# A Fourier-filter-and-snake-MLP kernel: forward transform with both sample parities in one 512-column matmul, and the filter's product in 512-wide pairs

## The chip, the cores and the metric

The kernel runs on one core of a Trainium2 chip. The metric is the device time of one execution in microseconds (us). TensorE (PE in the profile, PEld for its weight loads) multiplies, VectorE (DVE) and ScalarE (ACT) work elementwise, GpSimd (POOL) here issues the DMAs that change type, and SyncE (SP) issues the other DMAs.

## The reference, cut to what matters

The input has 8 batches of 3008 positions and 256 channels. Each batch is filtered along its positions by a real Fourier transform, and the result goes through a two-layer network with a snake activation:

```
X = np.fft.rfft(x, axis=1)
Y = X * (filt_r + 1j * filt_i)[None, :, :]
y = np.fft.irfft(Y, n=x.shape[1], axis=1)
h = y.reshape(B * S, D) @ w_in                 # 256 -> 2048
s = np.sin(alpha * h)
g = h + s * s / (alpha + 1e-09)
out = g @ w_out                                # 2048 -> 256
```

## The kernel before

The transform of length 3008 is split by parity. The even positions (r = 0) and the odd ones (r = 1) each have a transform of length 1504, done as matmuls with a table of cosines and sines, `dt_t`, that stays on the chip. 753 frequencies are kept, as 6 blocks of 128 (index i). Real and imaginary parts are p = 0 and p = 1. The odd half's twiddle factor and the filter are folded into coefficient tables once, at the start: P0 is the filter's even part, Q0 and P1 its odd part times the twiddle, each with a real and an imaginary table.

For each batch b:

- **x** is loaded (L205, L210) by GpSimd's queue, f32 to f16, into one tile for each parity, positions on the partitions in 12 chunks k (the last has 96 rows). The tile pool has two buffers of each.
- **Forward** (L226, L229): for each block i, part p and chunk k, one matmul 128x256 for the even samples into `psA` and one for the odd samples into `psB`, with the same weights `dt_t` loaded twice. 48 matmuls for one i, 288 for a batch. A PSUM tile of 512 columns holds both parts of one parity.
- **Copies** (L234, L235): ScalarE turns `psA` and `psB` into f16 tiles `asb` and `bsb` (two buffers each).
- **Product** (L247 to L253): VectorE forms four results z for each i, one for each output parity r and part p. Each takes four multiplications and three additions or subtractions of 128x256, 28 instructions for one i, 168 for a batch. The z tiles have one buffer.
- **Inverse** (L261): for each output parity r, 72 matmuls of 512 or 480 columns from z and the table `e_t` into `psy`, summed over all i and p; ScalarE copies them to `y` (L267).
- **Network** (L273 to L306): `psh` is y times w_in, ScalarE takes the sine, VectorE squares it in place (`v`, L283), and `pso` sums v times w_out (L292) and y times w_in·w_out (L299). VectorE copies `pso` to `o` and SyncE stores it.

At the start, VectorE makes the coefficient tables, for each i after a reversal of the filter on TensorE (`psrev`, L155) that VectorE copies out (L156, L157). The tiles of this part give their memory to those of the main loop, so the first load of x waits for all of it.

A scheduler sets the order on each engine from its own estimates, and each engine then keeps to that order. Between the last blocks of `pso` of one batch it places single forward matmuls of the next batch. Semaphores make an instruction wait for its operands.

Of the kernel before, what the change touches and what calls it, by code (L numbers as in the profile page):

```python
# [17 lines left out]
def kernel(  # L18
# [61 lines left out]
    P0re = cpool.tile([128, 6, C], FP16)  # L80
    P0im = cpool.tile([128, 6, C], FP16)
    Q0re = cpool.tile([128, 6, C], FP16)
    Q0im = cpool.tile([128, 6, C], FP16)
    P1re = cpool.tile([128, 6, C], FP16)
    P1im = cpool.tile([128, 6, C], FP16)
# [11 lines left out]
    with tc.tile_pool(name="init", bufs=1) as ipool:  # L97
# [68 lines left out]
        for i in range(6):  # L166
            wv = w3_t[:, 0, i:i + 1]
            wcv = w3_t[:, 1, i:i + 1]
            wsv = w3_t[:, 2, i:i + 1]
            nc.vector.tensor_tensor(out=gre, in0=fr_f[:, i, :], in1=fr_b[:, i, :], op=ALU.add)  # L170
            nc.vector.tensor_tensor(out=hre, in0=fr_f[:, i, :], in1=fr_b[:, i, :], op=ALU.subtract)
            nc.vector.tensor_tensor(out=gim, in0=fi_f[:, i, :], in1=fi_b[:, i, :], op=ALU.subtract)
            nc.vector.tensor_tensor(out=him, in0=fi_f[:, i, :], in1=fi_b[:, i, :], op=ALU.add)
            if i == 0:
                nc.vector.memset(gim[0:1, :], 0.0)
                nc.vector.memset(him[0:1, :], 0.0)
            nc.vector.tensor_scalar(out=P0re[:, i, :], in0=gre, scalar1=wv, scalar2=None, op0=ALU.mult)
# [5 lines left out]
            nc.vector.tensor_tensor(out=Q0re[:, i, :], in0=ta, in1=tb, op=ALU.add)
            nc.vector.tensor_tensor(out=Q0im[:, i, :], in0=tc_, in1=td, op=ALU.subtract)
            nc.vector.tensor_tensor(out=P1re[:, i, :], in0=ta, in1=tb, op=ALU.subtract)
            nc.vector.tensor_tensor(out=P1im[:, i, :], in0=tc_, in1=td, op=ALU.add)
# [10 lines left out]

    tok_chunks = [(0, 512), (512, 512), (1024, 480)]

    for b in range(B):  # L200
        xr_tiles = []
        for r in range(2):
            xt = xpool.tile([128, 12, C], FP16, name=f"x_{b}_{r}", tag=f"x{r}")
            base = x.offset + b * S * C + r * C
            nc.gpsimd.dma_start(  # L205
                out=xt[:, 0:11, :],
                in_=bass.AP(tensor=x.tensor, offset=base,
                            ap=[[2 * C, 128], [256 * C, 11], [1, C]]),
            )
            nc.gpsimd.dma_start(  # L210
                out=xt[0:96, 11, :],
                in_=bass.AP(tensor=x.tensor, offset=base + 1408 * 2 * C,
                            ap=[[2 * C, 96], [1, C]]),
            )
            xr_tiles.append(xt)
        Z = [[zpool.tile([128, 6, C], FP16, name=f"z_{b}_{r}_{p}", tag=f"z{r}{p}") for p in range(2)]
             for r in range(2)]
        for i in range(6):
            psA = fwdps.tile([128, 2, C], FP32, name=f"psA_{b}_{i}", tag="psA")
            psB = fwdps.tile([128, 2, C], FP32, name=f"psB_{b}_{i}", tag="psB")  # L220
            for p in range(2):
                col0 = p * NQP + 128 * i
                for k in range(12):
                    nrow = 128 if k < 11 else 96
                    lhs = dt_t[0:nrow, k, col0:col0 + 128]
                    nc.tensor.matmul(out=psA[:, p, :], lhsT=lhs,  # L226
                                     rhs=xr_tiles[0][0:nrow, k, :],
                                     start=(k == 0), stop=(k == 11))
# [7 lines left out]
            are, aim = asb[:, 0, :], asb[:, 1, :]
            bre, bim = bsb[:, 0, :], bsb[:, 1, :]
            t0 = abpool.tile([128, C], FP16, name=f"t0_{b}_{i}", tag="t0")
            t1 = abpool.tile([128, C], FP16, name=f"t1_{b}_{i}", tag="t1")
            for (zout, ops, c0, x0, c1, x1, c2, x2, c3, x3) in (  # L240
                (Z[0][0][:, i, :], 0, P0re, are, P0im, aim, Q0re, bre, Q0im, bim),
                (Z[0][1][:, i, :], 1, P0re, aim, P0im, are, Q0re, bim, Q0im, bre),
                (Z[1][0][:, i, :], 0, P1re, are, P1im, aim, P0re, bre, P0im, bim),
                (Z[1][1][:, i, :], 1, P1re, aim, P1im, are, P0re, bim, P0im, bre),
            ):
                sub = ALU.add if ops else ALU.subtract
# [96 lines left out]
```

## Time and profile before

| | |
|---|---|
| median of 5 runs | 1392.18 us (1391.09 to 1395.18) |
| profiled execution | 1390.42 us, of which the span from first to last instruction is 1388.6 us |
| PE busy | 1277.8 us (92%), 8524 matmuls |
| DVE busy | 752.8 us (54%), 2453 instructions |
| ACT busy | 562.8 us (41%), 962 instructions |
| DMA | mean 40 GB/s, q0 (GpSimd's) 24848 packets, 13.37 MB |
| mean granted clock of TensorE | 0.977 |

The busy times are sums over the whole span. The ends of matmuls are modelled and matmuls overlap, so a stretch of PE is read by the starts of its instructions. An idle time in the trace is the gap in front of an instruction, and the name behind it is what ended it.

### The profile page before, as it was taken

What the parts mean: (1) busy time and instruction counts of PE and PEld (TensorE: products, weight loads), DVE (VectorE), ACT (ScalarE), POOL (GpSimd) and SP (SyncE); (2) the same over time, 40 slices, a digit from 0 to 9 for tenths busy, and PEclk for the clock granted to TensorE, in tenths of its full rate; (3) what the DMA queues carried; (4) which work ended last, traced back from release to release, by engine and by line L of the source; (5) the groups of instructions that cost most, each with busy time, mean ns of one, the idle gap of its engine ahead of it and who ended that gap; (6) DMA issues with size and microseconds to landing.
All of it is one profiled execution on the core that took longest, in us unless ns stands there. A gap on an engine that the chain in (4) does not pass through costs nothing.

```text
span 1388.6 us, 21372 instructions
## 1 busy us (share of the span) xinstructions
PE 1277.8 (92%) x8524; PEld 819.1 (59%) x8524; DVE 752.8 (54%) x2453; ACT 562.8 (41%) x962; POOL 33.2 (2%) x53
## 2 busy tenths in 40 slices
PE   0629899989999999999999899998999999999998
PEld 0208465765568465775658565684657655684655
DVE  0757644495256753495355753486444952566534
ACT  0002546316361454416362264514463164613544
POOL 0110000000000000000000000000000000000000
PEclk9859999999999999999999999999999999999999
DMA  9542310030000310121000300103100000000101
GB/s 335 165 67 39 52 38 16 31 45 24 23 31 16 45 35 21 35 34 27 30 24 23 46 31 15 39 10 50 38 16 30 2 23 23 31 15 1 35 19 38
DMA packets 60501, 56.21 MB, mean 40 GB/s; under 512 B 6129, under 2 KB 59633, under 8 KB 59889
## 3 DMA queue, kind: packets, MB, share of 16 engines
q1 hardware_dynamic: 35552, 41.48, 8.6%
q0 software_dynamic: 24848, 13.37, 7.1%
q8 instruction: 66, 1.08, 0.4%
q14 instruction: 35, 0.28, 0.1%
HBM read 43.57 MB, written 24.64 MB: 49 GB/s over the span
## 4 chain that ended last, share of the span: by engine, by line
PE 72%; DVE 21%; SPq 2%; DMA 2%; issue 1%; ACT 1%; POOL 0%; ACTq 0%; DVEq 0%; POOLq 0%
PE pso L292 26%; PE psh L273 24%; PE psy L261 15%; PE pso L299 3%; DVE t L250 3%; DVE t L252 3%; DVE t L247 3%; DVE z L253 3%; DVE t L249 3%; DVE t L248 3%; DVE t L251 3%; SPq L99 2%; PE psB L229 2%; PE psA L226 1%; DMA tfwd<-in_filt_i_dram 1%
## 5 line engine op out<-in xcount | busy, mean ns | idle before, releaser
L279 ACT ACTIVATE v<-psh,alpha_t 128x512 f16<-128x512 f32 (+1 forms) x768 | 453.2, 718 | 174.5 <-PE psh L273 172.4
L283 DVE TENSOR_TENSOR v<-v 128x512 f16<-128x512 f16 (+1 forms) x768 | 321.4, 419 | 311.4 <-ACT v L279 285.5
L292 PE MATMUL pso<-w_out,v 128*128 128x256 f16 (+1 forms) x3072 | 443.6, 273 | 2.1 <-DVE o L306 1.5
L273 PE MATMUL psh<-y,w_in 128*128 128x512 f16 (+1 forms) x1536 | 418.2, 374 | 1.4 <-ACT v L279 1.4
L292 PEld LDWEIGHTS <-v 128*128 128x128 f16 (+1 forms) x3072 | 301.8, 99 | 180.9 <-DVE v L283 81.0
L261 PE MATMUL psy<-e_t,z 128*128 128x512 f16 (+1 forms) x1152 | 264.8, 382 | 29.2 <-DVE z L253 28.5
L226 PE MATMUL psA<-x,dt_t 128*128 128x256 f16 (+1 forms) x1152 | 255.4, 275 | 20.0 <-DMA x<-in_x_dram 20.0
L229 PE MATMUL psB<-x,dt_t 128*128 128x256 f16 (+1 forms) x1152 | 255.3, 274 | 1.1 <-DMA x<-in_x_dram 1.1
L273 PEld LDWEIGHTS <-w_in 128*128 128x128 f16 x1536 | 149.3, 97 | 101.2 <-issue 20.0
L261 PEld LDWEIGHTS <-z 128*128 128x128 f16 x1152 | 112.2, 99 | 161.8 <-DVE z L253 44.0
L306 DVE COPY o<-pso 128x256 f32<-128x256 f32 x192 | 81.5, 425 | 217.6 <-PE pso L299 217.3
L267 ACT CAST y<-psy 128x512 f16<-128x512 f32 (+1 forms) x96 | 54.6, 578 | 259.3 <-PE psy L261 259.3
L226 PEld LDWEIGHTS <-dt_t 128*128 128x128 f16 (+1 forms) x1152 | 112.9, 98 | 35.8 <-issue 21.6
L234 ACT CAST asb<-psA 128x512 f16<-128x512 f32 x48 | 28.1, 586 | 248.6 <-PE psA L226 136.5
L229 PEld LDWEIGHTS <-dt_t 128*128 128x128 f16 (+1 forms) x1152 | 113.5, 99 | 15.7 <-issue 1.4
L299 PE MATMUL pso<-m_t,y 128*128 128x256 f16 (+1 forms) x384 | 73.3, 273 | 0.0
L253 DVE TENSOR_TENSOR z<-t,t 128x256 f16<-128x256 f16 x192 | 54.6, 288 | 2.7
L249 DVE TENSOR_TENSOR t<-t,t 128x256 f16<-128x256 f16 x192 | 54.4, 286 | 1.8
L251 DVE TENSOR_TENSOR t<-t,t 128x256 f16<-128x256 f16 x192 | 54.4, 286 | 1.8
L247 DVE TENSOR_TENSOR t<-P0re,asb 128x256 f16<-128x256 f16 x96 | 27.5, 286 | 43.2 <-ACT asb L234 42.7
L119 PE MATMUL pst<-ident_t,w_in 128*128 128x128 f32 x32 | 10.6, 404 | 39.5 <-DMA w_in<-in_moe_w_in_dram 37.8
L234 ACT ACT_TABLE_LOAD x1 | 1.3, 1283 | 110.1 <-PE psA L226 110.1
(45 smaller groups left out, 378.2 us busy)
## 6 DMA issues: line engine op xcount, KB each, us to landing
out_dram<-o SPq DMA_DIRECT2D x176, 128.0 KB, 1.7
x<-in_x_dram POOLq DMA_DIRECT2D x16, 704.0 KB, 9.5
dt_t<-dt_tbl SPq DMA_DIRECT2D x1, 4608.0 KB, 15.6
e_t<-e_tbl SPq DMA_DIRECT2D x1, 4512.0 KB, 28.7
w_in<-in_moe_w_in_dram SPq DMA_DIRECT2D x1, 2048.0 KB, 7.5
w_out<-in_moe_w_out_dram SPq DMA_DIRECT2D x1, 2048.0 KB, 13.1
out_dram<-o SPq DMA_DIRECT2D x16, 96.0 KB, 1.7
w_in<-in_moe_w_in_dram POOLq DMA_DIRECT2D x1, 1024.0 KB, 28.9
```

The source lines that it names most:

```text
L226: nc.tensor.matmul(out=psA[:, p, :], lhsT=lhs, rhs=xr_tiles[0][0:nrow, k, :], start=(k == 0), stop=(k == 11))
L229: nc.tensor.matmul(out=psB[:, p, :], lhsT=lhs, rhs=xr_tiles[1][0:nrow, k, :], start=(k == 0), stop=(k == 11))
L249: nc.vector.tensor_tensor(out=t0, in0=t0, in1=t1, op=sub)
L251: nc.vector.tensor_tensor(out=t0, in0=t0, in1=t1, op=ALU.add)
L253: nc.vector.tensor_tensor(out=zout, in0=t0, in1=t1, op=sub)
L261: nc.tensor.matmul(out=psy[:, 0:n], lhsT=Z[r][p][:, i, cb * 128:cb * 128 + 128], rhs=e_t[:, p, i, m0:m0 + n], start=(i == 0 and p == 0), s ...
L273: nc.tensor.matmul(out=psh[:, 0:n], lhsT=w_in16[:, cb, jb * 128:jb * 128 + 128], rhs=ysb[:, cb, m0:m0 + n], start=(cb == 0), stop=(cb == 1),)
L279: nc.scalar.activation(out=vt[:, jb, 0:n], in_=psh[:, 0:n], func=AFT.Sin, scale=alpha_t[:, jb:jb + 1],)
L283: nc.vector.tensor_tensor(out=vt[:, jb, 0:n], in0=vt[:, jb, 0:n], in1=vt[:, jb, 0:n], op=ALU.mult,)
L292: nc.tensor.matmul(out=pso[0:tn, 0:C], lhsT=vt[:, jb, 128 * t:128 * t + tn], rhs=w_out2[:, jb, :], start=(jb == 0), stop=False,)
L299: nc.tensor.matmul(out=pso[0:tn, 0:C], lhsT=ysb[:, cb, m0 + 128 * t:m0 + 128 * t + tn], rhs=m_t[:, cb, :], start=False, stop=(cb == 1),)
L306: nc.vector.tensor_copy(out=osb[0:tn, :], in_=pso[0:tn, 0:C])
```

## The change

The two parity tiles of x become one tile of 12 chunks with 2 x 256 columns, loaded in rows twice as long. A forward matmul now has 512 columns, both parities at once, and the two PSUM tiles hold the real part and the imaginary part (`psRE`, `psIM`) instead of the even and the odd samples. There are 24 forward matmuls for one i instead of 48. The coefficient tables are stored side by side (`CR`, `CI`: for r = 0 [P0 | Q0], for r = 1 [P1 | P0]), which takes 12 more VectorE instructions at the start. A result z is now made by two multiplications and one addition or subtraction of 128x512 and one addition of 128x256: 16 instructions for one i instead of 28. The load of x for the next batch is written one batch ahead.

```
-            nc.vector.tensor_scalar(out=P0re[:, i, :], in0=gre, scalar1=wv, scalar2=None, op0=ALU.mult)
-            nc.vector.tensor_scalar(out=P0im[:, i, :], in0=gim, scalar1=wv, scalar2=None, op0=ALU.mult)
+            nc.vector.tensor_scalar(out=CR[0][:, i, 0, :], in0=gre, scalar1=wv, scalar2=None, op0=ALU.mult)
+            nc.vector.tensor_scalar(out=CR[1][:, i, 1, :], in0=gre, scalar1=wv, scalar2=None, op0=ALU.mult)
+            nc.vector.tensor_scalar(out=CI[0][:, i, 0, :], in0=gim, scalar1=wv, scalar2=None, op0=ALU.mult)
+            nc.vector.tensor_scalar(out=CI[1][:, i, 1, :], in0=gim, scalar1=wv, scalar2=None, op0=ALU.mult)
...
+    def load_x(b):
+        xt = xpool.tile([128, 12, 2, C], FP16, name=f"x_{b}", tag="x")
+        base = x.offset + b * S * C
+        nc.gpsimd.dma_start(
+            out=xt[:, 0:11, :, :],
+            in_=bass.AP(tensor=x.tensor, offset=base,
+                        ap=[[2 * C, 128], [256 * C, 11], [1, 2 * C]]),
+        )
...
+    x_pref = load_x(0)
     for b in range(B):
...
+        xr = x_pref
+        if b + 1 < B:
+            x_pref = load_x(b + 1)
...
-                    nc.tensor.matmul(out=psA[:, p, :], lhsT=lhs,
-                                     rhs=xr_tiles[0][0:nrow, k, :],
+                    nc.tensor.matmul(out=pst, lhsT=dt_t[0:nrow, k, col0:col0 + 128],
+                                     rhs=xr[0:nrow, k, :, :],
                                      start=(k == 0), stop=(k == 11))
-                    nc.tensor.matmul(out=psB[:, p, :], lhsT=lhs,
-                                     rhs=xr_tiles[1][0:nrow, k, :],
-                                     start=(k == 0), stop=(k == 11))
...
-            nc.scalar.copy(out=asb, in_=psA)
-            nc.scalar.copy(out=bsb, in_=psB)
+            nc.scalar.copy(out=resb, in_=psRE)
+            nc.scalar.copy(out=imsb, in_=psIM)
...
-                nc.vector.tensor_tensor(out=t0, in0=c0[:, i, :], in1=x0, op=ALU.mult)
-                nc.vector.tensor_tensor(out=t1, in0=c1[:, i, :], in1=x1, op=ALU.mult)
-                nc.vector.tensor_tensor(out=t0, in0=t0, in1=t1, op=sub)
-                nc.vector.tensor_tensor(out=t1, in0=c2[:, i, :], in1=x2, op=ALU.mult)
-                nc.vector.tensor_tensor(out=t0, in0=t0, in1=t1, op=ALU.add)
-                nc.vector.tensor_tensor(out=t1, in0=c3[:, i, :], in1=x3, op=ALU.mult)
-                nc.vector.tensor_tensor(out=zout, in0=t0, in1=t1, op=sub)
+            for r in range(2):
+                for p in range(2):
+                    x0, x1 = (resb, imsb) if p == 0 else (imsb, resb)
+                    sub = ALU.add if p else ALU.subtract
+                    w0 = abpool.tile([128, 2, C], FP16, name=f"w0_{b}_{i}_{r}_{p}", tag="w0")
+                    w1 = abpool.tile([128, 2, C], FP16, name=f"w1_{b}_{i}_{r}_{p}", tag="w1")
+                    nc.vector.tensor_tensor(out=w0, in0=CR[r][:, i, :, :], in1=x0, op=ALU.mult)
+                    nc.vector.tensor_tensor(out=w1, in0=CI[r][:, i, :, :], in1=x1, op=ALU.mult)
+                    nc.vector.tensor_tensor(out=w0, in0=w0, in1=w1, op=sub)
+                    nc.vector.tensor_tensor(out=Z[r][p][:, i, :], in0=w0[:, 0, :], in1=w0[:, 1, :], op=ALU.add)
```

VectorE, product of batch 0, before. A name such as t0_0_1_576 is tile t0 of batch 0 and block 1; t0_0_0_492 belongs to block 0.

```order
L248 TENSOR_TENSOR t1_0_0_493<-P1im_69,asb_0_0_488 128x256
L247 TENSOR_TENSOR t0_0_1_576<-P0re_64,asb_0_1_572 128x256 [waits Activation_49]
L249 TENSOR_TENSOR t0_0_0_492<-t0_0_0_492,t1_0_0_493 128x256 [waits DVE_49]
L248 TENSOR_TENSOR t1_0_1_577<-P0im_65,asb_0_1_572 128x256
L250 TENSOR_TENSOR t1_0_0_493<-P0re_64,bsb_0_0_489 128x256 [waits DVE_49]
L249 TENSOR_TENSOR t0_0_1_576<-t0_0_1_576,t1_0_1_577 128x256 [waits DVE_49]
L251 TENSOR_TENSOR t0_0_0_492<-t0_0_0_492,t1_0_0_493 128x256 [waits DVE_49]
L250 TENSOR_TENSOR t1_0_1_577<-Q0re_66,bsb_0_1_573 128x256 [waits DVE_49,Activation_49]
```

The same place with the change: from the first product of block 1 that needs the imaginary part to the end of its first two results, and on to the third.

```order
L242 TENSOR_TENSOR w1_0_1_0_0_533<-CI0_66,imsb_0_1_529 128x512 [waits Activation_49]
L241 TENSOR_TENSOR w0_0_1_0_1_538<-CR0_64,imsb_0_1_529 128x512 [waits DVE_49]
L243 TENSOR_TENSOR w0_0_1_0_0_532<-w0_0_1_0_0_532,w1_0_1_0_0_533 128x512 [waits DVE_49]
L242 TENSOR_TENSOR w1_0_1_0_1_539<-CI0_66,resb_0_1_528 128x512
L244 TENSOR_TENSOR z_0_0_0_444<-w0_0_1_0_0_532 128x256 [waits DVE_49]
L243 TENSOR_TENSOR w0_0_1_0_1_538<-w0_0_1_0_1_538,w1_0_1_0_1_539 128x512 [waits DVE_49]
L241 TENSOR_TENSOR w0_0_1_1_0_544<-CR1_65,resb_0_1_528 128x512 [waits DVE_49]
L244 TENSOR_TENSOR z_0_0_1_445<-w0_0_1_0_1_538 128x256 [waits DVE_49]
L242 TENSOR_TENSOR w1_0_1_1_0_545<-CI1_67,imsb_0_1_529 128x512
```

Before, two blocks stood interleaved, so that an instruction's operand came from the second instruction ahead of it. With the change two results of one block stand interleaved, again at a distance of two.

TensorE, first inverse matmuls of batch 0, before, from the tenth on (psy_0_0_0_0 and psy_0_0_0_512 are the first two of the three column chunks of y).

```order
L261 LDWEIGHTS z_0_0_1_435 [waits DVE_49]
L261 MATMUL psy_0_0_0_512_957<-e_t_59,z_0_0_1_435 128x512
L261 LDWEIGHTS z_0_0_0_434 [waits DVE_49]
L261 MATMUL psy_0_0_0_0_943<-e_t_59,z_0_0_0_434 128x512
L261 LDWEIGHTS z_0_0_0_434
L261 MATMUL psy_0_0_0_512_957<-e_t_59,z_0_0_0_434 128x512
```

With the change, from the eleventh on:

```order
L252 LDWEIGHTS z_0_0_0_444
L252 MATMUL psy_0_0_0_512_787<-e_t_59,z_0_0_0_444 128x512
L252 LDWEIGHTS z_0_0_0_444 [waits DVE_49]
L252 MATMUL psy_0_0_0_0_773<-e_t_59,z_0_0_0_444 128x512
L252 LDWEIGHTS z_0_0_1_445
L252 MATMUL psy_0_0_0_512_787<-e_t_59,z_0_0_1_445 128x512
L252 LDWEIGHTS z_0_0_0_444
L252 MATMUL psy_0_0_0_512_787<-e_t_59,z_0_0_0_444 128x512
L252 LDWEIGHTS z_0_0_1_445 [waits DVE_49]
L252 MATMUL psy_0_0_0_0_773<-e_t_59,z_0_0_1_445 128x512
```

Before, 16 matmuls of other blocks stood ahead of the one that waits for the real z of block 5, and 10 more ahead of the one that waits for the imaginary z. Now 11 stand ahead of the first and 2 between the two.

GpSimd's queue, loads of x for batches 0 and 1, before:

```order
L210 DMA x_0_0_428<-in_x_dram 96x256
L205 DMA x_0_1_431<-in_x_dram 128x11x256
L210 DMA x_0_1_431<-in_x_dram 96x256
L205 DMA x_1_0_2126<-in_x_dram 128x11x256
L210 DMA x_1_0_2126<-in_x_dram 96x256
```

And with the change:

```order
L207 DMA x_0_438<-in_x_dram 96x512
L202 DMA x_1_441<-in_x_dram 128x11x512
L207 DMA x_1_441<-in_x_dram 96x512
L202 DMA x_2_1956<-in_x_dram 128x11x512 [waits DMASW2_49,DMASW1_49,PE_49]
L207 DMA x_2_1956<-in_x_dram 96x512
```

In both, two batches are asked for at once at the start, and the third waits for TensorE to be done with the first.

## Rows read from the trace of the kernel before

**Rows 1.** The page, part 4: shares of the chain that ended last

```profile
PE 72%; DVE 21%; SPq 2%; DMA 2%; issue 1%; ACT 1%; POOL 0%; ACTq 0%; DVEq 0%; POOLq 0%
```

**Rows 2.** Groups by line: busy us, mean ns of one, idle before and its releaser

```profile
L283 DVE TENSOR_TENSOR v<-v 128x512 f16<-128x512 f16 (+1 forms) x768 | 321.4, 419 | 311.4 <-ACT v L279 285.5
...
L261 PE MATMUL psy<-e_t,z 128*128 128x512 f16 (+1 forms) x1152 | 264.8, 382 | 29.2 <-DVE z L253 28.5
...
L235 ACT CAST bsb<-psB 128x512 f16<-128x512 f32 x48 | 28.2, 589 | 21.1 <-DVE t L252 21.1
```

**Rows 3.** Timeline, PE, batch 1: start us, us, line, count, idle before

```profile
267.38 0.27 PE L226 MATMUL psA<-x,dt_t 128*128 128x256 f16 x1
...
296.68 2.39 PE L261 MATMUL psy<-e_t,z 128*128 128x512 f16 x9
301.36 1.69 PE L261 MATMUL psy<-e_t,z 128*128 128x512 f16 x7 [2.28 <-DVE z L253]
...
307.38 9.63 PE L261 MATMUL psy<-e_t,z 128*128 128x512 f16 x45 [0.19 <-DVE z L253]
```

**Rows 4.** Timeline, VectorE, batch 1: interleaved, then dependent, then the last imaginary part

```profile
284.01 0.28 DVE L251 TENSOR_TENSOR t<-t,t 128x256 f16<-128x256 f16 x1
284.22 0.28 DVE L248 TENSOR_TENSOR t<-P0im,asb 128x256 f16<-128x256 f16 x1
...
288.30 0.29 DVE L251 TENSOR_TENSOR t<-t,t 128x256 f16<-128x256 f16 x1
288.62 0.29 DVE L252 TENSOR_TENSOR t<-Q0im,bsb 128x256 f16<-128x256 f16 x1
...
307.04 0.29 DVE L253 TENSOR_TENSOR z<-t,t 128x256 f16<-128x256 f16 x1
```

**Rows 5.** Timeline, VectorE, setup: multiplications and additions, f32 operands

```profile
90.06 0.34 DVE L182 TENSOR_SCALAR td<-hre,w_t 128x256 f32<-128x256 f32 x1
90.32 0.41 DVE L183 TENSOR_TENSOR Q0re<-ta,tb 128x256 f16<-128x256 f32 x1
90.66 0.42 DVE L184 TENSOR_TENSOR Q0im<-tc__312,td 128x256 f16<-128x256 f32 x1
```

**Rows 6.** Timeline, PE, batch 0: an inverse without waits, the next stage's start

```profile
206.10 12.79 PE L261 MATMUL psy<-e_t,z 128*128 128x512 f16 x60
218.73 0.59 PE L273 MATMUL psh<-y,w_in 128*128 128x512 f16 x2
```

**Rows 7.** Timeline, PE, batch 0: first and later block of its first inverse

```profile
136.22 2.10 PE L261 MATMUL psy<-e_t,z 128*128 128x512 f16 x9
...
146.57 9.63 PE L261 MATMUL psy<-e_t,z 128*128 128x512 f16 x45 [0.19 <-DVE z L253]
```

**Rows 8.** Timeline, all engines, first copy and product of batch 1

```profile
270.59 0.59 ACT L234 CAST asb<-psA 128x512 f16<-128x512 f32 x1 [11.97 <-PE psA L226]
...
271.21 0.29 DVE L247 TENSOR_TENSOR t<-P0re,asb 128x256 f16<-128x256 f16 x1 [3.21 <-ACT asb L234]
```

**Rows 9.** Timeline, all engines, between two batches: a slot of forward matmuls

```profile
262.10 0.27 PE L226 MATMUL psA<-x,dt_t 128*128 128x256 f16 x1
...
262.78 1.91 PE L292 MATMUL pso<-w_out,v 128*128 128x256 f16 x16
```

**Rows 10.** Timeline, all engines, start: last reversal copy, loads of x, first forward matmuls

```profile
80.17 0.41 DVE L157 COPY fi_b<-psrev 128x256 f32<-128x256 f32 x1
...
92.38 1.09 POOL L205 DMA_DIRECT2D x<-in_x_dram  x1 [42.64 <-DVE P1im L186]
```

**Rows 11.** Timeline, PE, start: the same stretch, first forward matmuls

```profile
99.80 2.72 PE L226 MATMUL psA<-x,dt_t 128*128 128x256 f16 x12 [20.02 <-DMA x<-in_x_dram]
103.62 2.72 PE L229 MATMUL psB<-x,dt_t 128*128 128x256 f16 x12 [1.09 <-DMA x<-in_x_dram]
```

**Rows 12.** Busy time in stretches: PE, PEld, DVE, ACT, POOL, granted clock, DMA, GB/s

```profile
99.80:103.60 3.80, 2.72 (x12) 1.73 (x13) 0.00 (x0) 0.00 (x0) 0.00 (x0) 0.50 1.45 196
103.60:110.00 6.40, 6.38 (x37) 4.67 (x37) 0.00 (x0) 0.00 (x0) 0.00 (x0) 0.61 1.46 198
```

More of the change, by code (lines that the diff above doesn't have):

```diff
@@ L79 @@
     nc.sync.dma_start(out=w3_t, in_=w3_dram.ap())
[L80 to L85, printed above, removed]
+    CR = [cpool.tile([128, 6, 2, C], FP16, name=f"CR{r}") for r in range(2)]
+    CI = [cpool.tile([128, 6, 2, C], FP16, name=f"CI{r}") for r in range(2)]
     w_in16 = cpool.tile([128, 2, DFF], FP16)
@@ L182 @@
             nc.vector.tensor_scalar(out=td, in0=hre, scalar1=wsv, scalar2=None, op0=ALU.mult)
[L183 to L186, printed above, removed]
+            nc.vector.tensor_tensor(out=CR[0][:, i, 1, :], in0=ta, in1=tb, op=ALU.add)
+            nc.vector.tensor_tensor(out=CI[0][:, i, 1, :], in0=tc_, in1=td, op=ALU.subtract)
+            nc.vector.tensor_tensor(out=CR[1][:, i, 0, :], in0=ta, in1=tb, op=ALU.subtract)
+            nc.vector.tensor_tensor(out=CI[1][:, i, 0, :], in0=tc_, in1=td, op=ALU.add)
     xpool = ctx.enter_context(tc.tile_pool(name="xp", bufs=2))
@@ L198 @@
     tok_chunks = [(0, 512), (512, 512), (1024, 480)]
-    for b in range(B):
[L201 to L215, printed above, removed]
+    def load_x(b):
[6 more added lines that the diff above has]
+        )
+        nc.gpsimd.dma_start(
+            out=xt[0:96, 11, :, :],
+            in_=bass.AP(tensor=x.tensor, offset=base + 1408 * 2 * C,
+                        ap=[[2 * C, 96], [1, 2 * C]]),
+        )
+        return xt
+    x_pref = load_x(0)
+    for b in range(B):
+        xr = x_pref
+        if b + 1 < B:
+            x_pref = load_x(b + 1)
         Z = [[zpool.tile([128, 6, C], FP16, name=f"z_{b}_{r}_{p}", tag=f"z{r}{p}") for p in range(2)]
@@ L218 @@
         for i in range(6):
-            psA = fwdps.tile([128, 2, C], FP32, name=f"psA_{b}_{i}", tag="psA")
-            psB = fwdps.tile([128, 2, C], FP32, name=f"psB_{b}_{i}", tag="psB")
-            for p in range(2):
+            psRE = fwdps.tile([128, 2, C], FP32, name=f"psRE_{b}_{i}", tag="psRE")
+            psIM = fwdps.tile([128, 2, C], FP32, name=f"psIM_{b}_{i}", tag="psIM")
+            for p, pst in ((0, psRE), (1, psIM)):
                 col0 = p * NQP + 128 * i
@@ L224 @@
                     nrow = 128 if k < 11 else 96
-                    lhs = dt_t[0:nrow, k, col0:col0 + 128]
-                    nc.tensor.matmul(out=psA[:, p, :], lhsT=lhs,
-                                     rhs=xr_tiles[0][0:nrow, k, :],
+                    nc.tensor.matmul(out=pst, lhsT=dt_t[0:nrow, k, col0:col0 + 128],
+                                     rhs=xr[0:nrow, k, :, :],
                                      start=(k == 0), stop=(k == 11))
-                    nc.tensor.matmul(out=psB[:, p, :], lhsT=lhs,
-                                     rhs=xr_tiles[1][0:nrow, k, :],
-                                     start=(k == 0), stop=(k == 11))
@@ L232 @@
-            asb = abpool.tile([128, 2, C], FP16, name=f"asb_{b}_{i}", tag="asb")
-            bsb = abpool.tile([128, 2, C], FP16, name=f"bsb_{b}_{i}", tag="bsb")
-            nc.scalar.copy(out=asb, in_=psA)
-            nc.scalar.copy(out=bsb, in_=psB)
[L236 to L246, printed above, removed]
-                nc.vector.tensor_tensor(out=t0, in0=c0[:, i, :], in1=x0, op=ALU.mult)
-                nc.vector.tensor_tensor(out=t1, in0=c1[:, i, :], in1=x1, op=ALU.mult)
-                nc.vector.tensor_tensor(out=t0, in0=t0, in1=t1, op=sub)
-                nc.vector.tensor_tensor(out=t1, in0=c2[:, i, :], in1=x2, op=ALU.mult)
-                nc.vector.tensor_tensor(out=t0, in0=t0, in1=t1, op=ALU.add)
-                nc.vector.tensor_tensor(out=t1, in0=c3[:, i, :], in1=x3, op=ALU.mult)
-                nc.vector.tensor_tensor(out=zout, in0=t0, in1=t1, op=sub)
+            resb = abpool.tile([128, 2, C], FP16, name=f"resb_{b}_{i}", tag="resb")
@@ new lines @@
+            imsb = abpool.tile([128, 2, C], FP16, name=f"imsb_{b}_{i}", tag="imsb")
+            nc.scalar.copy(out=resb, in_=psRE)
[10 more added lines that the diff above has]
+                    nc.vector.tensor_tensor(out=Z[r][p][:, i, :], in0=w0[:, 0, :], in1=w0[:, 1, :], op=ALU.add)
```

## The prediction

> **What bounds the kernel now.** The shares of the chain come first: PE has 72% of it, but DVE 21% [rows 1], so the product on VectorE ends some wait in every batch. The groups by line say which: the inverse transform stands idle for 29.2 us in front of its matmuls, 28.5 of them released by z [rows 2]. The timeline of TensorE in batch 1 shows the place. The last 268 forward matmuls run without a gap from 267.38 to 296.68, 0.1093 us each. Then the inverse starts, does nine matmuls, and stalls three times for z, until its block of 45 starts at 307.38 [rows 3].
>
> The idle column understates the stall, since the modelled ends of matmuls reach into it. I take it from starts. Sixty inverse matmuls without waits take 218.73 - 206.10 = 12.63 us [rows 6]. 36 of them have 512 columns and 24 have 480, so they equal 58.5 of 512 columns, and one of these takes 0.2159 us. The 27 matmuls between the first and the block of 45 (22 of 512, 5 of 480, worth 26.7) need 5.76 us. They took 307.38 - 296.68 = 10.70, so 4.94 were waiting [rows 3]. In batch 0 it was 146.57 - 136.22 = 10.35, hence 4.59 [rows 7]. The other six stretches have 10.69 to 11.05, and the eight together 85.6. Less 8 x 5.76 = 46.1, that is **39.5 us of waiting for z**.
>
> Why z is late: 48 forward matmuls of one block i take 48 x 0.1093 = 5.25 us. VectorE starts two instructions of 256 columns 0.20 to 0.21 us apart when two blocks are interleaved, and 0.32 apart when each needs the one before [rows 4]. 28 instructions so take 5.9 us at best, and VectorE falls behind block by block: it runs from 271.21 [rows 8] to the last imaginary part at 307.04 + 0.29 [rows 4], 36 us for 154 instructions. TensorE is not held up in the forward part, since its PSUM tiles come free in time.
>
> **The change part by part.**
>
> *Product.* For a block there are 12 instructions of 512 columns and 4 of 256. No row shows two f16 instructions of 512 columns back to back with nothing to wait for. The nearest are f32 ones of 256 columns: 0.42 long, as the squares of 512 f16 columns are [rows 2], and they start 0.34 apart [rows 5]. I take 0.34, and 0.21 for the narrow ones: 12 x 0.34 + 4 x 0.21 = **4.92 us**. Bounds: below, the spacing cannot go under the narrow one, 16 x 0.21 = 3.4; above, if each waited for the one ahead, 0.42 + 0.04 and 0.29 + 0.04, 12 x 0.46 + 4 x 0.33 = 6.84. I stay at 4.92, because in the new order each operand comes from the second instruction ahead, as it does in the interleaved rows.
>
> TensorE needs 24 x 0.2159 = 5.18 us for a block, so VectorE is now the faster one by 0.26, and no backlog grows. What is late next is the tail of block 5. Let T be the start of the first inverse matmul. Before, ScalarE started 0.37 after the start of the last matmul of psA (28 matmuls after 267.38 end at 270.44, the last of psA starts 0.22 earlier, the copy starts at 270.59 [rows 8]). The last matmul now starts at T - 0.22 and is 0.11 longer, so the copy of the imaginary part starts at T + 0.26. It takes 0.59 [rows 2], and VectorE starts 0.03 later: T + 0.88. The new order has four wide instructions ahead of the real z, which ends at T + 0.88 + 1.36 + 0.29 = T + 2.53. TensorE follows 0.05 later (307.33 to 307.38 before), but has 11 matmuls to do first, until T + 2.37: a wait of 0.2. The imaginary z starts 0.21 + 0.68 after the real one's start and lets TensorE go at T + 3.47. It is ready for it three matmuls after T + 2.58, at T + 3.23: a wait of 0.24. Together 0.45 a batch, 3.6 in all. **Gain 39.5 - 3.6 = 35.9.** The bounds are 39.5 and, with 6.84 a block, a loss (third rival). The copies of one block take about 1.2 us of ScalarE in 5.2, and the square and the sines start only after the inverse, so they hide no cost.
>
> *Forward.* Between two batches single matmuls fill slots in which TensorE would wait for the copy of pso; a slot is 262.78 - 262.10 = 0.68 us [rows 9]. Five of 256 columns fill 0.55 of it, three of 512 fill 0.65. So 12 of the 144 fit where 20 of the 288 stood, and the rest of a batch is 132 x 0.2159 = 28.50 in place of 29.30. **Gain 0.80 x 7 = 5.6**, and 0.3 in batch 0, which has no slots. Halving the weight loads gains nothing more; they already lie beside the matmuls, or the forward part would not run at 0.1093.
>
> *Start.* Twelve more multiplications at 0.26 [rows 5] are 3.1 us of VectorE. The reversal copies are paced by their small loads, and the last stands at 80.17 [rows 10]. In the new order 48 instructions stand behind that copy instead of 37, so nearly all 3.1 us come behind it, and VectorE runs there without a pause. The load of x follows the last one, at 95.5 instead of 92.38 [rows 10]. Before, TensorE started 7.4 us after the issue, when the even half was there, and the odd half came 11.2 after it [rows 11]. One load now brings both halves. Bounds: 7.4 if its rows count, since there are as many as in one half, and 11.2 if its bytes count. I take 11.2, the rate of both halves: start at 106.7 instead of 103.62, with 12 cold matmuls not yet done.
>
> The granted clock was 0.50 up to 103.6. Its mean was 0.61 in the next 6.4 us [rows 12], so it rose from 1.2 to 2.4 GHz after 5.0 of them, 8.8 after the first matmul. If it again rises 5 us after the start, the loss is 3.1 + 12 x 0.109 = 4.4. If it takes 8.8, the 3.8 further us at half rate cost 1.9 more, 6.3. I take **a loss of 5.0**, with ends at 0.6 (load in 7.4: 0.7 earlier than 103.62, less 1.3) and 6.3. Later loads wait for the same buffers as before, though written one batch ahead, and go out a whole inverse and network stage before they are wanted.
>
> **Sum.** 35.9 + 5.6 + 0.3 - 5.0 = 36.8 us. The profiled execution took 1390.42 (1388.6 of span and 1.8 around it), which becomes 1353.6. The median stands 1.8 above it, so I predict **1355 us**. This likeliest case reaches from 1347 (no waits left, the early load) to 1362.
>
> **The rivals.**
>
> *VectorE stays the bound.* If an instruction started only when the one ahead had ended, a block would take 12 x 0.42 + 4 x 0.29 = 6.2 us. In batch 1 block 0's imaginary part is ready for VectorE at 267.38 + 12 x 0.2159 + 0.88 = 270.85. The last imaginary z would end at 270.85 + 5 x 6.2 + 3.1 = 304.95, and TensorE would go on at 305.0 instead of 307.38: 2.4 x 8 = 19 gained, 5 lost at the start, **1378 us**. For it: no row shows wide pairs. Against it: in the rows narrow ones start 0.20 to 0.21 apart and last 0.28, and f32 ones start 0.34 apart and last 0.42 [rows 4, 5]. Chance 0.12, with all spacings between 0.36 and 0.42.
>
> The Trainium skill speaks for this rival: in "VectorE: DVE Perf Modes", section "The DRAIN you can't avoid", it says that "the next op does not start until the 8-stage pipe empties", with semaphores or without, though it adds that an op that is not held starts earlier. By the first half the change would be worth 14 us, by the second 37. The trace's starts, 0.07 to 0.08 ahead of the end of the one before, agree with the second.
>
> *The start costs more.* The loads of batches 0 and 1 are in flight together. If the first lands only when both have, 2.9 MB (four loads of 128x11x256 f16 before) at 196 GB/s [rows 12] and about 3 us of latency (18 us) put TensorE's start at 113.5, 6.8 later than taken: **1362 us**. Against it: before, the even half was there 3.8 us ahead of the odd one. Chance 0.08.
>
> *Slower: each wide instruction waits for the one ahead.* With 6.84 a block the last z of batch 1 comes at 270.85 + 34.2 + 3.4, and TensorE goes on at 308.5, 1.1 later than before. With the start that is 8 x 1.1 + 5 = 14 lost, **1406 us**. It decides from 6.5 us a block on. For it: the dependent rows with 0.32 [rows 4]; against it: the distance of two in the new order. Chance 0.06.
>
> *Nothing gained.* If the stall were the delay of the last link alone and not VectorE's pace, it would stay, and 5.9 from the forward part would go against 5.0 at the start: **1391 us**. Against it: 36 us of VectorE beside 31 of TensorE. Chance 0.04.
>
> **How the numbers follow.** The forecast has 0.70. The range of 1347 to 1372 holds it, the costlier start and the nearer half of the first rival. About 0.2% is what a measurement here tells from no change, 2.8 us. Forecast, first and second rival are faster by more: 0.90. The fourth is the same, 0.04. The third is slower, 0.06.
>
> **What would show it.** In the profile after, the forward matmuls should start 0.216 apart; the gap in front of the inverse should be under 1 us a batch in place of nearly 5; VectorE's wide instructions should start 0.34 apart and pause for the copies of ScalarE; DVE should nearly vanish from the chain; and the first forward matmul should start near 106.7. A batch should take 4.94 - 0.45 + 0.80 = 5.3 us less from inverse to inverse. It is wrong if wide instructions stand 0.40 or more apart, if z still releases the inverse late, or if the forward matmuls need 0.23 each.

## The result, and the profile after

The kernel with the change takes **1353.28 us** (median of 8 runs, 1352.04 to 1354.04). The kernel before took 1393.9 us beside it (15 runs, 1390.63 to 1396.44). The ratio is 0.971, with an interval of 0.9699 to 0.9722. The forecast was 1355.0. The medians are 40.6 us apart. In the profiled executions the span went from 1388.6 to 1350.6 us, 38.0 less, where the prediction's sum was 36.8. Beside the experiments, runs of the kernel before went from 1390.38 us at a mean granted clock of 0.978 to 1396.33 at 0.969; the profiled one had 0.977 and the change's eight 0.980 or 0.981.

The page after, busy time and shares of the chain:

```profile
PE 1261.5 (93%) x7372; PEld 705.0 (52%) x7372; DVE 685.9 (51%) x1889; ACT 565.1 (42%) x962; POOL 20.1 (1%) x37
...
PE 91%; DVE 3%; SPq 2%; DMA 2%; ACT 1%; issue 0%; ACTq 0%; DVEq 0%; POOLq 0%
```

VectorE's share of the chain fell from 21% [rows 1] to 3%. The groups by line tell what took its place (columns as in [rows 2]):

```profile
L252 PE MATMUL psy<-e_t,z 128*128 128x512 f16 (+1 forms) x1152 | 255.5, 375 | 0.6
...
L228 PE MATMUL psRE<-x,dt_t 128*128 128x512 f16 x576 | 138.7, 383 | 28.1 <-DMA x<-in_x_dram 28.1
...
L242 DVE TENSOR_TENSOR w<-CI,imsb 128x512 f16<-128x512 f16 x96 | 40.5, 422 | 31.4 <-ACT imsb L234 31.4
```

The inverse's 29.2 us of idle time in front of it are 0.6 now, and VectorE waits for ScalarE's copies, 31.4 us in all: in the product it now runs ahead of TensorE, whose forward results these copies bring. The 28.1 us in front of the forward matmuls are one gap, the wait for the first x. TensorE in batch 1, the inverse and the start of the next stage (columns: start, us, line, count):

```profile
297.38 15.81 PE L252 MATMUL psy<-e_t,z 128*128 128x512 f16 x72
313.02 2.57 PE L264 MATMUL psh<-y,w_in 128*128 128x512 f16 x10
```

The inverse is one row of 72 in place of the four stretches of [rows 3]. At 0.2159 us for 512 columns its 72 matmuls (48 of 512 and 24 of 480, worth 70.5) need 15.22 us. They took 313.02 - 297.38 = 15.64, so 0.42 of waiting is left. It is the same in all eight batches, and from batch 1 on a batch takes 154.06 us.

VectorE in the same batch, one block of the product:

```profile
287.87 0.43 DVE L242 TENSOR_TENSOR w<-CI,imsb 128x512 f16<-128x512 f16 x1 [0.27 <-ACT imsb L234]
288.21 0.42 DVE L241 TENSOR_TENSOR w<-CR,imsb 128x512 f16<-128x512 f16 x1
288.55 0.42 DVE L243 TENSOR_TENSOR w<-w,w 128x512 f16<-128x512 f16 x1
288.88 0.42 DVE L242 TENSOR_TENSOR w<-CI,resb 128x512 f16<-128x512 f16 x1
289.22 0.29 DVE L244 TENSOR_TENSOR z<-w 128x256 f16<-128x256 f16 x1
289.42 0.42 DVE L243 TENSOR_TENSOR w<-w,w 128x512 f16<-128x512 f16 x1
...
293.06 0.42 DVE L242 TENSOR_TENSOR w<-CI,imsb 128x512 f16<-128x512 f16 x1 [0.27 <-ACT imsb L234]
```

Wide instructions start 0.33 to 0.34 apart, narrow ones 0.20. The block goes from 287.87 to 293.06, 5.19 us, of which 0.27 is the pause for the copy: 4.92 of work.

The start, all engines, from the last reversal copy to the first forward matmuls:

```profile
81.18 0.41 DVE L154 COPY fi_b<-psrev 128x256 f32<-128x256 f32 x1
...
95.52 0.42 DVE L185 TENSOR_TENSOR CI<-tc__310,td 128x256 f16<-128x256 f32 x1
96.57 1.09 POOL L202 DMA_DIRECT2D x<-in_x_dram  x1 [46.73 <-DVE CI L185]
...
108.91 4.63 PE L228 MATMUL psRE<-x,dt_t 128*128 128x512 f16 x12 [28.11 <-DMA x<-in_x_dram]
113.38 2.75 PE L228 MATMUL psIM<-x,dt_t 128*128 128x512 f16 x12
```

The load is issued 4.2 us later than before and TensorE starts 9.1 later than [rows 11] has it, though before it then waited again for the odd half. The first inverse starts at 141.92 instead of 136.22 [rows 7], **5.7 us later**.

### The profile page after: what moved, and what is told of

It is laid out like the page before. It is cut to its first block, busy times and chain, and to the rows that moved or that the text cites. A ratio compares the mean times of both kernels' runs of the same rounds, so it can differ in the third digit from the quotient of the medians.

```text
span 1350.6 us, 18474 instructions
## 1 busy us (share of the span) xinstructions
PE 1261.5 (93%) x7372; PEld 705.0 (52%) x7372; DVE 685.9 (51%) x1889; ACT 565.1 (42%) x962; POOL 20.1 (1%) x37
## 4 chain that ended last, share of the span: by engine, by line
PE 91%; DVE 3%; SPq 2%; DMA 2%; ACT 1%; issue 0%; ACTq 0%; DVEq 0%; POOLq 0%
PE pso L283 26%; PE psh L264 25%; PE psy L252 16%; PE psRE L228 9%; PE psIM L228 9%; PE pso L290 3%; SPq L96 2%; DMA x<-in_x_dram 1%; PE psrev L152 1%; DMA tfwd<-in_filt_i_dram 1%; PE pst L116 1%; DMA w_in<-in_moe_w_in_dram 1%; ACT v L270 0%; DVE w L242 0%; PE psm L126 0%; DVE w L243 0%
## 5 line engine op out<-in xcount | busy, mean ns | idle before, releaser
L252 PE MATMUL psy<-e_t,z 128*128 128x512 f16 (+1 forms) x1152 | 255.5, 375 | 0.6
L228 PEld LDWEIGHTS <-dt_t 128*128 128x128 f16 (+1 forms) x1152 | 112.8, 98 | 159.0 <-issue 32.2
L228 PE MATMUL psRE<-x,dt_t 128*128 128x512 f16 x576 | 138.7, 383 | 28.1 <-DMA x<-in_x_dram 28.1
L228 PE MATMUL psIM<-x,dt_t 128*128 128x512 f16 x576 | 132.3, 379 | 0.0
L233 ACT CAST resb<-psRE 128x512 f16<-128x512 f32 x48 | 28.1, 585 | 129.2 <-PE psRE L228 65.2
L243 DVE TENSOR_TENSOR w<-w,w 128x512 f16<-128x512 f16 x192 | 80.4, 419 | 0.0
L234 ACT CAST imsb<-psIM 128x512 f16<-128x512 f32 x48 | 28.1, 585 | 109.4 <-PE psIM L228 109.4
L242 DVE TENSOR_TENSOR w<-CI,imsb 128x512 f16<-128x512 f16 x96 | 40.5, 422 | 31.4 <-ACT imsb L234 31.4
L244 DVE TENSOR_TENSOR z<-w 128x256 f16<-128x256 f16 x192 | 54.8, 285 | 0.3
L241 DVE TENSOR_TENSOR w<-CR,resb 128x512 f16<-128x512 f16 x96 | 40.3, 420 | 25.9 <-ACT resb L233 25.9
```

The source lines that it names most:

```text
L228: nc.tensor.matmul(out=pst, lhsT=dt_t[0:nrow, k, col0:col0 + 128], rhs=xr[0:nrow, k, :, :], start=(k == 0), stop=(k == 11))
L242: nc.vector.tensor_tensor(out=w1, in0=CI[r][:, i, :, :], in1=x1, op=ALU.mult)
L243: nc.vector.tensor_tensor(out=w0, in0=w0, in1=w1, op=sub)
L244: nc.vector.tensor_tensor(out=Z[r][p][:, i, :], in0=w0[:, 0, :], in1=w0[:, 1, :], op=ALU.add)
L252: nc.tensor.matmul(out=psy[:, 0:n], lhsT=Z[r][p][:, i, cb * 128:cb * 128 + 128], rhs=e_t[:, p, i, m0:m0 + n], start=(i == 0 and p == 0), s ...
```

## The experiments

The theory: VectorE's pace on the product made the inverse wait; the change brings it under TensorE's pace, and so nearly all of the wait goes. The main rival: VectorE's pace stays the same and the forward part alone brings the gain, or the waits are a delay at the end of the chain that any order has.

**Wide forward matmuls, narrow product.** The six narrow tables and the 28 instructions of 128x256 are put back behind the 512-column forward matmuls.

```
-   nc.vector.tensor_tensor(out=w0, in0=CR[r][:, i, :, :], in1=x0, op=ALU.mult)
...
+   nc.vector.tensor_tensor(out=t0, in0=c0[:, i, :], in1=x0, op=ALU.mult)
+   nc.vector.tensor_tensor(out=t1, in0=c1[:, i, :], in1=x1, op=ALU.mult)
...
```

> The forward part, the loads of x and the copies as changed; the product as before (28 instructions of 256 columns a block, tables as before, so no added setup instructions). Theory (VectorE's pace in the product set the waits before the inverse, and the wide product removed them): VectorE again needs 5.9 to 6.0 us a block against 5.18 on TensorE, 4 to 5 us of waiting for z come back in each batch, the time is 1385 to 1397 us, about that of before. Rival (the gain comes from half as many forward matmuls and weight loads): 1350 to 1362 us.

Measured: 1374.45 us (1373.24 to 1374.78), ratio 0.9855 (0.9833 to 0.9876). TensorE in batch 1:

```profile
297.13 2.10 PE L261 MATMUL psy<-e_t,z 128*128 128x512 f16 x9
301.04 1.69 PE L261 MATMUL psy<-e_t,z 128*128 128x512 f16 x7 [1.80 <-DVE z L253]
303.87 12.18 PE L261 MATMUL psy<-e_t,z 128*128 128x512 f16 x56 [1.15 <-DVE z L253]
315.89 2.57 PE L273 MATMUL psh<-y,w_in 128*128 128x512 f16 x10
```

The stalls are back, so the product removes them. But the time fell between the two expectations. The 72 matmuls take 18.76 us here, 3.54 of them waiting, where it was 4.95 before (316.85 - 296.68 = 20.17, less 15.22) and 0.42 with the whole change. Eight times 3.54 - 0.42 is 25.0. The load of x goes out earlier, without the 12 added table instructions: the first forward matmul stands at 105.17 and the first inverse at 138.56, 3.4 before the changed kernel's. 1353.3 + 25.0 - 3.4 = 1374.9, against 1374.45 measured. My expectation had taken the waits of before whole and forgotten the start. Why the same 28 instructions wait 1.4 less a batch, with real and imaginary parts copied in turn rather than even and odd samples, was not tried apart. The rows of VectorE in batch 1 point at its order: of the product's first 150 starts, 36 came 0.32 to 0.33 us after the one ahead in the kernel before and 23 here, in place of the 0.20 to 0.21 of most others, and 13 such starts are worth 1.6 us.

**Wide product, narrow forward matmuls.** Each 512-column matmul is done as two of 256, all chunks of one parity first.

```
-   for k in range(12):
-       nc.tensor.matmul(out=pst, ..., rhs=xr[0:nrow, k, :, :], ...)
+   for h in range(2):
+       for k in range(12):
+           nc.tensor.matmul(out=pst[:, h, :], ..., rhs=xr[0:nrow, k, h, :], ...)
```

> The product and the loads as changed; each 512-column forward matmul taken apart again into two of 256 columns with their own weight loads, the even samples of a part first, then the odd ones. Theory: TensorE needs 5.25 us a block instead of 5.18 and the slots between batches hold less, some 6 us in all: 1357 to 1362 us, still with waits under 1 us a batch. Rival (fewer forward matmuls are the gain): 1385 us or more.

Measured: 1359.19 us (1358.65 to 1359.93), ratio 0.9747 (0.9726 to 0.9768).

```profile
297.93 15.81 PE L253 MATMUL psy<-e_t,z 128*128 128x512 f16 x72
313.57 1.24 PE L265 MATMUL psh<-y,w_in 128*128 128x512 f16 x5
```

The inverse takes 15.64 us, as with the whole change: the product alone removes the waits. What is missing to 1353.28 is 5.9 us, the size of the sum's forward term (5.6 + 0.3), but it is not split as the sum has it: a batch takes 154.93 us from inverse to inverse, 0.87 more than with the whole change and 6.1 in seven. In batch 0 it takes 33.75 us from the first forward matmul to the first inverse (107.84 to 141.59), 0.7 more, and the first matmul came 1.1 earlier in this execution. The two halves overlap: 20 us alone, 35 alone, 40 together, for less waiting is left to remove once either is in.

**One buffer of the product's intermediate tiles.** Work and widths stay; w0 and w1 come from a pool of one buffer, so that two results can't stand interleaved.

```
+   wpool = ctx.enter_context(tc.tile_pool(name="wp", bufs=1))
-   w0 = abpool.tile([128, 2, C], FP16, ..., tag="w0")
+   w0 = wpool.tile([128, 2, C], FP16, ..., tag="w0")
```

> The changed kernel with one buffer instead of two for the wide tiles w0 and w1, so that the two results of a block can't be interleaved on VectorE; instructions and sizes are the same. Theory: sums and z then start 0.46 us after their operand, a block takes 0.21 + 0.34 + 0.46 + 0.46 = 1.47 a result, 5.9 us in all, which is over TensorE's 5.18; the last z comes some 4 us later in each batch and the time is 1375 to 1390 us, though VectorE's busy time is the same. Rival (the number of instructions is what counts, not their spacing): 1353 to 1357 us.

Measured: 1381.62 us (1379.93 to 1383.79), ratio 0.9908 (0.9885 to 0.9932). VectorE, one result, and TensorE in batch 1:

```profile
286.25 0.29 DVE L245 TENSOR_TENSOR z<-w 128x256 f16<-128x256 f16 x1
286.46 0.42 DVE L243 TENSOR_TENSOR w<-CI,imsb 128x512 f16<-128x512 f16 x1
286.79 0.42 DVE L242 TENSOR_TENSOR w<-CR,resb 128x512 f16<-128x512 f16 x1
287.25 0.42 DVE L244 TENSOR_TENSOR w<-w,w 128x512 f16<-128x512 f16 x1
287.70 0.29 DVE L245 TENSOR_TENSOR z<-w 128x256 f16<-128x256 f16 x1
```

```profile
302.93 2.54 PE L253 MATMUL psy<-e_t,z 128*128 128x512 f16 x11
308.44 14.71 PE L253 MATMUL psy<-e_t,z 128*128 128x512 f16 x61 [2.97 <-DVE z L245]
322.98 1.24 PE L265 MATMUL psh<-y,w_in 128*128 128x512 f16 x5
```

An instruction that needs the one ahead starts 0.45 to 0.46 after it (286.79 to 287.25 to 287.70), 0.03 to 0.04 after its end, in place of 0.34. A result takes 1.45 us and a block 5.8, more than TensorE's 5.18. The 72 matmuls of batch 1 take 20.05 us, 4.83 more than the 15.22, but this is not all waiting: for 3.41 us of it the granted clock was 0.50 (1.2 GHz; columns as in [rows 12]).

```profile
309.55:312.96 3.41, 3.41 (x10) 1.21 (x9) 3.06 (x9) 0.59 (x1) 0.00 (x0) 0.50 1.19 193
```

In batches 3 to 6, where the clock stayed up, they take 18.35 to 18.37, so VectorE's pace costs 3.1 us a batch, where it is 0.42 with two buffers. In the other four the clock fell during the inverse, and these took 7.7 us longer in all. Waits (8 x 2.7), clock and a first inverse 1.1 later make 30.6 of the 31.0 us between the profiled spans. So most of what the 16 instructions are worth hangs on the order at a distance of two: the same work in dependent order gives 28 of the 40 us back in the medians.

**Half of the product left out.** The multiplication with CI and the sum behind it are left out, so z is no longer the filter's product.

```
-   nc.vector.tensor_tensor(out=w1, in0=CI[r][:, i, :, :], in1=x1, op=ALU.mult)
-   nc.vector.tensor_tensor(out=w0, in0=w0, in1=w1, op=sub)
```

> Leaves out half of the product: the multiplication with CI and the subtraction or addition behind it, so 8 instructions a block instead of 16 (z is not the reference's). Theory: VectorE is already faster than TensorE in the forward part, so its 130 us less of work are worth at most the 0.42 us that the inverse still waits in each batch: 1349 to 1353 us. Rival (VectorE's pace still sets the time): 1340 us or less.

Measured: 1349.71 us (1348.7 to 1350.2), ratio 0.9678 (0.9653 to 0.9703).

```profile
296.58 15.38 PE L249 MATMUL psy<-e_t,z 128*128 128x512 f16 x72
311.80 1.46 PE L261 MATMUL psh<-y,w_in 128*128 128x512 f16 x6
```

The inverse takes 15.22, no wait at all. With half of VectorE's product gone only 3.6 us are won, 8 x 0.42 = 3.4: in the changed kernel VectorE's pace no longer bounds anything but the tail of the last block.

The loss at the start was more than the prediction had. Three runs took it apart.

**The first load in pieces.** The load of the first 11 chunks of x for batch 0 is split.

```
+   for (k0, k1) in (((0, 2), (2, 5), (5, 8), (8, 11)) if b == 0 else ((0, 11),)):
        nc.gpsimd.dma_start(
-           out=xt[:, 0:11, :, :],
+           out=xt[:, k0:k1, :, :],
```

> The start term. In the changed kernel the load of x for batch 0 is issued at 96.57, lands as a whole at 108.9, and TensorE starts then. Here it is split by chunks into four loads (2, 3, 3 and 3 of the first 11 chunks) and the tail, of the same bytes; the load of batch 1 is as it was. If TensorE waits for the landing of bytes, the first matmuls start near 101 to 102, run as the pieces land, and the first block of 12 ends near 109.5 in place of 113.4: 3 to 5 us less, 1349 us (1348 to 1351). If the latency of a load or the load of batch 1, which is in flight beside it, sets the landing, the last piece comes no earlier and the pieces bring less than 1.5 us: 1352 to 1354.

Measured: 1349.46 us (1349.19 to 1350.8), ratio 0.9682 (0.9668 to 0.9697). TensorE at the start:

```profile
100.85 1.01 PE L229 MATMUL psRE<-x,dt_t 128*128 128x512 f16 x2 [19.97 <-DMA x<-in_x_dram]
103.01 1.44 PE L229 MATMUL psRE<-x,dt_t 128*128 128x512 f16 x3 [1.15 <-DMA x<-in_x_dram]
105.36 1.44 PE L229 MATMUL psRE<-x,dt_t 128*128 128x512 f16 x3 [0.91 <-DMA x<-in_x_dram]
107.35 2.03 PE L229 MATMUL psRE<-x,dt_t 128*128 128x512 f16 x4 [0.55 <-DMA x<-in_x_dram]
109.17 4.68 PE L229 MATMUL psIM<-x,dt_t 128*128 128x512 f16 x12
113.70 2.76 PE L229 MATMUL psRE<-x,dt_t 128*128 128x512 f16 x12
```

TensorE does follow the pieces, and the first 12 matmuls are done 4.2 us earlier (109.17 against 113.38). But the next 12 still take 4.53 us here, where they took 2.60. The granted clock tells why (columns as in [rows 12]):

```profile
101.00:105.00 4.00, 2.30 (x5) 0.55 (x4) 0.00 (x0) 0.00 (x0) 0.86 (x2) 0.50 1.13 166
105.00:110.00 5.00, 4.08 (x9) 1.19 (x9) 0.00 (x0) 0.55 (x1) 0.00 (x0) 0.50 1.22 202
110.00:115.00 5.00, 5.00 (x18) 1.94 (x17) 0.91 (x3) 1.90 (x3) 0.00 (x0) 0.69 1.16 193
```

It stays at 0.50 (1.2 GHz) through the matmuls with gaps between them and rises near 113.1, in the changed kernel near 112.8. So 1.9 of the 4.2 us are given back, and the first inverse starts at 139.64, 2.3 earlier. The profiled spans differ by 1.8 and the medians by 3.8; the three executions that were not profiled had spans of 1347.1 to 1347.6 where this one had 1348.8, so what is given back differs between executions.

**The added table instructions on ScalarE.** The 12 second copies of P0 are made by ScalarE.

```
-   nc.vector.tensor_scalar(out=CR[1][:, i, 1, :], in0=gre, scalar1=wv, ...)
+   nc.scalar.copy(out=CR[1][:, i, 1, :], in_=CR[0][:, i, 0, :])
```

> The start term, its other half. The twelve added table instructions at the start go from VectorE to ScalarE (copies of the tables' first halves), which is idle there. If VectorE's chain behind the last reversal copy holds the load of x, the load is issued near 93.5 in place of 96.57, the first forward matmul comes 3 us earlier, near 105.8, and the time is 1350 us (1349.5 to 1351). If the copies on ScalarE end last in their place, or the reversal's loads pace the setup, nothing is gained: 1353.

Measured: 1348.75 us (1348.58 to 1349.91), ratio 0.9677 (0.9661 to 0.9693).

```profile
80.57 0.41 DVE L154 COPY fi_b<-psrev 128x256 f32<-128x256 f32 x1
...
91.72 0.43 DVE L185 TENSOR_TENSOR CI<-tc__310,td 128x256 f16<-128x256 f32 x1
92.78 1.09 POOL L202 DMA_DIRECT2D x<-in_x_dram  x1 [42.64 <-DVE CI L185]
```

```profile
104.84 4.87 PE L228 MATMUL psRE<-x,dt_t 128*128 128x512 f16 x12 [24.64 <-DMA x<-in_x_dram]
```

The load goes out 3.8 us earlier and the forward part starts 4.1 earlier. The span is 3.9 shorter. VectorE's chain does hold the load. From the last reversal copy to the last table it takes 91.72 - 80.57 = 11.15 us, and 95.52 - 81.18 = 14.34 in the changed kernel: the 12 instructions cost 3.2, nearly the 3.1 of their own spacing. The other 0.6 is the reversal copy itself, which differs between executions: in the profiles of the change and of the first six experiments it starts anywhere from 80.16 to 81.62.

**An early load.** On top of that, x of even batches has memory of its own, outside what the setup uses, and batch 0 is loaded at the beginning.

```
-   xpool = ctx.enter_context(tc.tile_pool(name="xp", bufs=2))   # after the setup
+   xpool = ctx.enter_context(tc.tile_pool(name="xp", bufs=1))   # before it, even batches
+   x_pref = load_x(0, xpool)
...
+   xpool2 = ctx.enter_context(tc.tile_pool(name="xp2", bufs=1)) # after it, odd batches
```

> The start taken out of the chain. The tile of x for even batches gets memory of its own that the setup doesn't use (two pools of one buffer in place of one pool of two), so that the load for batch 0 goes out at the beginning; the twelve table instructions are on ScalarE as in the experiment before. The load competes with the tables' loads, whose last part releases the setup at 37.8: up to 6 us later. The forward matmuls of blocks 0 and 1 can then run while VectorE still makes coefficient tables; the product starts when these are ready, near 93 to 98, and six blocks of 4.92 put the first inverse near 122 to 128 in place of 141.9: 1334 to 1341 us. If something else holds the forward part (the order on TensorE, the PSUM tiles, memory that the setup still uses), it starts as in the changed kernel less the 3 us: 1349 or more.

Measured: **1332.85 us** (1331.75 to 1333.14), ratio 0.956 (0.9545 to 0.9574).

```profile
87.66 0.41 DVE L172 COPY fi_b<-psrev 128x256 f32<-128x256 f32 x1
88.13 4.67 PE L230 MATMUL psRE<-x,dt_t 128*128 128x512 f16 x12 [0.85 <-DVE fi_b L172]
...
121.18 4.05 PE L254 MATMUL psy<-e_t,z 128*128 128x512 f16 x18
126.59 11.52 PE L254 MATMUL psy<-e_t,z 128*128 128x512 f16 x54 [1.36 <-DVE z L246]
137.95 1.46 PE L266 MATMUL psh<-y,w_in 128*128 128x512 f16 x6
```

The forward part starts 0.06 us behind the end of the last reversal copy, beside VectorE's table work. The setup itself is later, since the load shares the DMA engines with the tables: its first matmul waits for w_in until 44.01 where it started at 38.23 in the run before, and its last table stands at 98.81 where it stood at 91.72. Even so the first inverse starts 16.9 us earlier than there, and 15.7 of the span go. In batch 0 alone VectorE is behind again, 1.55 us, because its product starts late, at 100.01. This is the fastest version, 20 us under the change and 16 under the run before, and a little better than the expectation's 1334.

## Why the prediction was right, point by point

Counted by the same starts, 1388.6 - 1350.6 = 38.0 is made of the following.

- **The waits for z**: predicted 35.9, measured 38.0, of which some 36.2 are waits. What is left came out as said (0.42 a batch for 0.45). The first 72 matmuls of the eight inverses before took 41.4 us more than 8 x 15.22, not 39.5, and the 1.8 that the working lacks lie in one batch. It has the other six stretches of 27 matmuls at 10.69 to 11.05, but the last batch's is 12.47 (1253.40 to 1265.87), so the eight are 87.4 and not 85.6. And this 1.8 is no wait for z. In the last batch the granted clock fell to 0.50 (1.2 GHz) for 6.83 us, while the inverse worked between its waits and behind them (TensorE's rows, then stretches with columns as in [rows 12]):

```profile
1253.40 2.40 PE L261 MATMUL psy<-e_t,z 128*128 128x512 f16 x9
1258.07 2.36 PE L261 MATMUL psy<-e_t,z 128*128 128x512 f16 x7 [2.28 <-DVE z L253]
1261.43 14.06 PE L261 MATMUL psy<-e_t,z 128*128 128x512 f16 x56 [1.00 <-DVE z L253]
...
1258.93:1265.76 6.83, 5.83 (x15) 1.91 (x14) 6.59 (x31) 0.00 (x0) 0.00 (x0) 0.50 0.00 0
1265.76:1275.33 9.57, 9.57 (x48) 4.41 (x46) 2.37 (x9) 2.81 (x5) 0.00 (x0) 1.00 0.00 0
```

  The seven matmuls from 1258.07 on last 2.36 us there, and 1.69 in batch 1 [rows 3]. In three more batches the clock fell for 3.41 us in the stretch of the waits, at 460.21, 620.64 and 1098.51, and these inverses took as long as batch 1's. In the changed kernel the clock doesn't fall again between its rise at the start and the last microseconds. So the change took away 1.8 us of lower clock along with the waits, a term that the prediction had at nothing.
- **The product's block**: 4.92 us, as worked out from f32 rows of 256 columns. The choice between 3.4 and 6.84 by the distance of operands was the step on which all rested, and the one-buffer run shows the other side of it: 4.92 at a distance of two, 5.8 at one.
- **The forward part**: predicted 0.80 a batch, 5.6 in seven, and 0.3 in batch 0. From the first inverse to the last one's start the seven batches are 37.4 us shorter, 31.7 of it in the inverses, so the rest is 5.7, 0.81 a batch. In batch 0 the narrow forward matmuls take 0.7 longer up to the inverse (33.75 for 33.01), where 0.3 was said; the clock also rose 0.7 later after the first matmul there, worth some 0.4. A batch is 159.40 - 154.06 = 5.34 shorter; 5.3 was forecast.
- **The start**: a loss of 4.7 was forecast (5.0 less batch 0's 0.3), 5.7 was measured. The step that was too small is the place of the first forward matmul, 106.7 forecast and 108.91 found. The last reversal copy came 1.0 later (81.18 for 80.17), which is within what executions differ: with the same setup it came at 80.16 in the run with narrow forward matmuls, and the load went out at 95.55 as forecast. The load then took 12.3 us from issue to start where the two halves had taken 11.2. Of the two bounds bytes were the right one; rows would have given 7.4. The clock partly made up for it: the first 12 matmuls took 4.47 us, since it rose 3.8 us after the start and not 5.
- 38.0 + 5.7 - 5.7 = 38.0, as the span has it, against 35.9 + 5.6 - 4.7 = 36.8. The two terms that were off, the lower clock with 1.8 and the start with 1.0, ran against each other, and that part of the close sum is luck. The waits, VectorE's block and the forward part came out by the mechanism that was said. The median of 1392.18 from which the forecast counted was of five runs, and that of all fifteen is 1393.9, so the measured medians lie further apart than the sum.

The rivals: *VectorE stays the bound* had 1378 for 6.2 us a block. The one-buffer run has less than that, 5.8, and yet 1382 us: the rival's price lacks the 7.7 us that the fallen clock cost there. Its condition, wide instructions that start only when the one ahead has ended, didn't hold in the change. *The start costs more* fell: TensorE started 2.2 us later than taken, with the load of batch 1 in flight, and not 6.8. *Each wide instruction waits* and *nothing gained* fell with the row of 4.92 and the 0.42.

The rule in the Trainium skill, "VectorE: DVE Perf Modes", section "The DRAIN you can't avoid", had two readings. The trace after agrees with the one for an instruction that isn't held: 0.42 long and 0.335 apart, a start 0.08 ahead of the end of the one before. In the one-buffer run an instruction that waits for the result of the one just ahead starts 0.03 to 0.04 after that end.

## What to carry to other kernels

When one engine's pace per block is a little over the next one's, the backlog shows up once, in front of the stage that needs all blocks; compare the two paces per block, work out which side of the line the change puts them, and anything beyond that is worth little (3.6 us for half of the work here). Fewer and wider instructions helped far less here when no independent ones lay between dependent ones, so count the buffers before counting the instructions. A wait can cost more than its own length, as the granted clock may fall in it: read the clock of a stretch before calling all of it waiting. And look at what the setup's memory holds up: 16 us lay in giving the first load a place of its own (1348.75 to 1332.85).

## What was not expected of the hardware

- 1408 rows of 2 KB and a tail took 12.3 us from issue to the first matmul (11.6 to 12.4 in the other runs with this load at the start). Before, the same bytes as two loads of half the row length were there 11.2 us after the issue of the first. Longer rows were no gain here.
- Matmuls that start early but with gaps left the granted clock at 0.50 for longer: 1.9 us of the 4.2 that the split load had won.
- The granted clock fell to 0.50 where the inverse waited: in four of eight batches before and in four with one buffer, but not in every batch with such a wait, and in no batch of the other runs.
- The wide forward matmuls alone, with the old product, cut the waits from 4.95 to 3.54 us a batch. The change of order on VectorE is the likely cause (23 late starts where there were 36), and it is only argued.
